# Attention's tensor part, its eviction and its use dealt out over successive steps, and left-over block products spread over three phases

## Chip, core and metric

One core of one Trainium2 chip. The metric is device time in microseconds (us) of one execution. The profiled span is some 2 us below the device time. An eviction is a read of matmul results out of PSUM, the memory that matmuls write to, by ACT or DVE; idle time before an instruction is shown in square brackets, with what ended it. Engines: PE (TensorE matmul), PEld (its weight loads), DVE (VectorE), ACT (ScalarE), SP (issues DMAs).

## The reference, cut to what matters

```python
# B=8 batches, H=8 heads, S=512 tokens, 32 states, D=64
scores  = scale * x @ state.T;  a  = softmax(scores);  xread = a @ state
scores2 = scale * state @ x.T;  a2 = softmax(scores2); sread = a2 @ x
x = concat([xread, sread], axis=2), laid out as (8 * 544, 512)
h = x @ w_in            # w_in 512 x 2048, 64-bit
g = h * cos(h)
return g @ w_out        # w_out 2048 x 512, 64-bit
```

## The kernel before

Instructions keep the order in which the program gives them, engine by engine; waits between engines are set from the tiles that instructions read and write. The main loop has 128 token steps (16 tiles of 128 hidden columns for each batch) and 16 steps for the states of all batches. In a step, `hidden` is two matmul calls into a PSUM buffer `h`, of which there are two. The gate follows: ACT (copy that adds a large constant, to round), DVE (`gate2`), ACT (Abs, sine; `gate3`), DVE (product, `gate4`).

The output product of two batches is done as seven block products in place of eight, in four phases of eight steps. One product per step goes into the MAIN half of an accumulator, in the fourth phase a fifth one into the SIDE half as well; the last two, `p7` and `p4`, are left over and go into the SIDE half during the next pair. Each tile's product follows its hidden matmul by three steps (`LAG`).

```python
at  = aps.tile([P, 2, S], F32, name="at")       # PSUM, attention
acc = ops.tile([P, 2, 2, S], F32, name="o")     # PSUM: MAIN, SIDE x 2 banks each

def tokens(self, k):                  # tensor part and eviction together
    for c in range(NC):
        self.turn_x(k, c, at[:, k % 2])
    nc.scalar.copy(self.xT[:, k], at[:, k % 2])
...
def output(t):
    if t.phase == 0:
        if product(MAIN, a11, t, i): keep_product(pr.u, MAIN)   # ACT reads MAIN
        if pr.before: p7(pr.before, i)                          # SIDE
    if t.phase == 1:
        last = product(MAIN, a12, t, i)
        if pr.before: p4(pr.before, i)                          # SIDE
        for ch in range(2 if last else 0):
            plus(pr.o, MAIN, ch, pr.u)                          # DVE reads MAIN
            ...
    # phase 2: MAIN alone.  phase 3: MAIN and SIDE, then the evictions
...
for step, t in enumerate(tiles()):    # conversions of weights cut
    hidden(t); gate(t); gate2(t); gate3(t)
    go(2 * s)                         # an attention part, whatever its engine
    if len(line) >= LAG: output(line.pop(0))
    gate4(t); sums(t)
    go(2 * s + 1)                     # the next attention part
    sums2(t)
```

The weights come as 64-bit numbers. Each of 20 blocks is turned into 32 bits by two ACT and four DVE instructions; 14 of them fall into steps 0 to 17.

## Time and profile before

| | before |
|---|---|
| device time, median of 3 runs | 955.45 us (951.56 to 956.37) |
| span profiled | 952.9 us |
| PE, DVE, ACT busy | 84%, 51%, 43% |
| mean granted PE clock | 0.951 |

PE is the fullest engine, but a share of busy time is an average. The prediction below shows the lines: the busy time of each stretch, the waits, and one wait as the timeline has it. The stretches are cut at the first hidden matmul of steps 0, 18, 32, 64, 96 and 128; steps 0 to 31 are pair 0, and so on by 32.

### The profile page before, as it was taken

Reading aid. Unit: us, or ns where it says so; the run is one execution under the profiler, and the core shown is the slowest. Engines: PE = TensorE matmul, PEld = TensorE weight load, DVE = VectorE, ACT = ScalarE, POOL = GpSimd, SP = SyncE. Lnnn points to the kernel's source line nnn. Section 1 sums busy time; section 2 is a strip of 40 time slices with the busy share of each in tenths; the row PEclk is TensorE's granted clock in tenths of the full one; section 3 lists DMA queues with packets and bytes.
Section 4 is the critical chain, followed back from the end, with each engine's and each line's share of the span. In section 5 each row is a group of like instructions: output and inputs, shape, how many; then the busy total and the mean of one; then the engine's idle time right before and its main releaser. Section 6 shows DMA issues by size and latency. Waiting matters only on the chain.

```text
span 952.9 us, 7331 instructions
## 1 busy us (share of the span) xinstructions
PE 797.4 (84%) x2720; PEld 350.9 (37%) x2720; DVE 482.4 (51%) x725; ACT 410.4 (43%) x634; POOL 3.1 (0%) x10
## 2 busy tenths in 40 slices
PE   3367667857998989689999899589989899899997
PEld 1133223323443434233433344234434343354454
DVE  2865866866644243756463326566442436643521
ACT  1555575554345424444444344543454335422312
POOL 1000000000000000000000000000000000000000
PEclk9879979989998999889999999799999999999999
DMA  5463223102000210202010301120000105001101
GB/s 132 150 182 133 90 87 88 22 1 45 0 14 10 41 26 1 44 1 45 0 23 0 67 1 22 23 44 1 11 11 1 22 1 133 1 0 23 22 10 35
DMA packets 110499, 37.17 MB, mean 39 GB/s; under 512 B 102464, under 2 KB 102464, under 8 KB 110464
## 3 DMA queue, kind: packets, MB, share of 16 engines
q1 hardware_dynamic: 109248, 36.19, 16.3%
q10 hardware_dynamic: 1088, 0.26, 0.2%
q8 instruction: 21, 0.34, 0.2%
q0 software_dynamic: 128, 0.26, 0.1%
q14 instruction: 14, 0.11, 0.0%
HBM read 27.79 MB, written 8.91 MB: 39 GB/s over the span
## 4 chain that ended last, share of the span: by engine, by line
PE 65%; DVE 19%; ACT 12%; issue 1%; DMA 1%; SPq 0%; DVEq 0%; ACTq 0%
PE o L464 33%; PE h L417 22%; PE at L274 4%; PE o L572 3%; DVE q L426 3%; ACT q L432 3%; DVE held L470 2%; ACT q L431 2%; DVE g_all L441 2%; DVE g_all L438 2%; PE at L354 1%; ACT q L423 1%; ACT xT L315 1%; DVE xT L293 1%; ACT L310 1%
## 5 line engine op out<-in xcount | busy, mean ns | idle before, releaser
L417 PE MATMUL h<-aT,sw 128*128 128x512 f32 x512 | 261.3, 635 | 9.6 <-ACT sw L386 7.9
L464 PE MATMUL o<-g_all,w_out 128*128 128x512 f32 x512 | 237.8, 604 | 6.1 <-ACT held L476 3.5
L426 DVE SCALAR_TENSOR_TENSOR q<-q,h 128x512 f32<-128x512 f32 (+1 forms) x144 | 93.9, 652 | 253.3 <-ACT q L423 253.0
L423 ACT ACTIVATE q<-h 128x512 f32<-128x512 f32 (+1 forms) x144 | 82.4, 572 | 274.6 <-PE h L417 274.6
L464 PE MATMUL o<-g_all,s 128*128 128x512 f32 x384 | 176.9, 596 | 3.5 <-ACT held L476 2.7
L431 ACT ACTIVATE q<-q 128x512 f32<-128x512 f32 (+1 forms) x144 | 87.3, 606 | 179.2 <-DVE q L426 179.2
L438 DVE TENSOR_TENSOR g_all<-h,q 128x512 f32<-128x512 f32 (+1 forms) x144 | 94.8, 658 | 132.0 <-ACT q L432 131.9
L417 PEld LDWEIGHTS h<-aT,sw 128*128 128x128 f32 x512 | 98.6, 202 | 136.5 <-issue 111.4
L464 PEld LDWEIGHTS o<-g_all,w_out 128*128 128x128 f32 x512 | 97.0, 195 | 130.3 <-issue 117.3
L464 PEld LDWEIGHTS o<-g_all,s 128*128 128x128 f32 x384 | 71.3, 191 | 92.8 <-issue 85.0
L432 ACT ACTIVATE q<-q,halfpi 128x512 f32<-128x512 f32 (+1 forms) x144 | 100.5, 698 | 4.5
L274 PE MATMUL at<-w_in,stT 64*32 64x512 f32 (+1 forms) x512 | 42.3, 705 | 54.1 <-ACT xT L315 41.7
L441 DVE TENSOR_TENSOR g_all<-g_all 128x512 f32<-128x512 f32 x128 | 83.2, 688 | 3.2
L470 DVE SCALAR_TENSOR_TENSOR held<-o,held 128x512 f32<-128x512 f32 x40 | 25.9, 687 | 41.8 <-PE o L464 41.5
L386 ACT COPY sw<-at 128x1024 f32<-128x1024 f32 (+1 forms) x32 | 31.6, 987 | 24.9 <-PE at L274 24.9
L572 PE MATMUL o<-w_out,g_all 128*128 128x512 f32 x64 | 31.3, 621 | 6.4 <-DVE w_out L221 4.1
L274 PEld LDWEIGHTS at<-w_in,stT 64*32 64x32 f32 x512 | 6.4, 112 | 80.1 <-ACT xT L315 47.5
L417 PE MATMUL h<-sT,w_in 128*128 128x256 f32 x128 | 30.2, 379 | 0.0
L417 PEld LDWEIGHTS h<-sT,w_in 128*128 128x128 f32 x128 | 24.3, 190 | 10.1 <-issue 6.7
L249 PE MATMUL at<-ident,x_b 128*128 128x128 f32 x112 | 17.6, 281 | 10.5 <-ACT xT L256 6.3
L249 PEld LDWEIGHTS at<-ident,x_b 128*128 128x128 f32 x112 | 13.9, 144 | 27.7 <-ACT xT L256 12.1
L488 DVE STREAM_TRANSPOSE ot<-held 128x512 f32<-128x512 f32 x32 | 22.3, 696 | 1.3 <-DMA out_dram<-ot 1.2
(72 smaller groups left out, 397.5 us busy)
## 6 DMA issues: line engine op xcount, KB each, us to landing
out_dram<-ot SPq DMA_DIRECT2D x136, 64.0 KB, 2.0
x_b<-in_x_dram SPq DMA_DIRECT2D x32, 256.0 KB, 4.4
g_all<-in_moe_w_out_dram SPq DMA_DIRECT2D x8, 1024.0 KB, 4.9
g_all<-in_moe_w_in_dram SPq DMA_DIRECT2D x6, 1024.0 KB, 5.1
g_all<-in_moe_w_in_dram SPq DMA_DIRECT2D x4, 512.0 KB, 7.3
x_b<-in_moe_w_out_dram SPq DMA_DIRECT2D x1, 1024.0 KB, 5.8
xT<-in_moe_w_out_dram SPq DMA_DIRECT2D x1, 1024.0 KB, 7.9
s<-in_state_dram ACTq DMA_DIRECT2D x4, 64.0 KB, 5.2
```

The costliest lines, as they stand in the source:

```text
L274: nc.tensor.matmul(out=(to[j] if to else at[:, j])[Ns * k:Ns * k + Ns, 0:n], lhsT=w[D * j:D * j + D, self.b, Ns * k:Ns * k + Ns], rhs=r(sl ...
L386: nc.scalar.copy(sw_of[self.b, nt][:, :, c0:c1], at[:, :, 0:c1 - c0])
L417: nc.tensor.matmul(out=t.hp, lhsT=t.lhs(i), rhs=t.rhs(i), start=(i == 0), stop=(i == t.kn - 1))
L423: nc.scalar.activation(t.q, t.hp, func=ACTF.Copy, bias=MAGIC)
L426: nc.vector.scalar_tensor_tensor(out=t.q, in0=t.q, scalar=MAGIC, in1=t.hp, op0=ALU.subtract, op1=ALU.subtract)
L431: nc.scalar.activation(t.q, t.q, func=ACTF.Abs)
L432: nc.scalar.activation(t.q, t.q, func=ACTF.Sin, bias=halfpi, scale=-TWO_PI)
L438: nc.vector.tensor_tensor(t.g, t.hp, t.q, op=ALU.mult)
L441: nc.vector.tensor_tensor(out, a, b, op=ALU.subtract)
L464: nc.tensor.matmul(out=acc[:, bank, ch], lhsT=w[:, i, P * ch:P * ch + P], rhs=g.g, start=(i == 0), stop=(i == NH - 1))
L470: nc.vector.scalar_tensor_tensor(out=out[:, ch], in0=acc[:, bank, ch], scalar=TWO_PI, in1=b[:, ch], op0=ALU.mult, op1=ALU.add)
L572: nc.tensor.matmul(out=acc[:, MAIN, i], lhsT=t.g[:, P * i:P * i + P], rhs=w_out[:, :, t.f, :], start=(n == 0), stop=(n == NF - 1))
```

## The change

Its intent: attention's matmuls, the evictions of their results and their use go into different lists, so that each stands at a fitting place of a step (matmuls ahead of `hidden`, an eviction behind the first gate instruction, vector work in the hole while ACT computes) and the use comes a step or more later. The left-over products are popped from a list in two of three steps of phases 0 to 2, in place of every step of phases 0 and 1. Cut to its core:

```diff
         def tokens(self, k):
             for c in range(NC):
                 self.turn_x(k, c, at[:, k % 2])
+
+        def tokens_kept(self, k):
             nc.scalar.copy(self.xT[:, k], at[:, k % 2])
...                                    # turn, keep3 and products alike
+        def products(self, nt, bank=None, c0=0, c1=WC):
+            to = at if bank is None else acc[:, bank]     # pair 0: SIDE is idle
...
         if t.phase == 0:
             if product(MAIN, a11, t, i):
+                pr.u = Held()
                 keep_product(pr.u, MAIN)
-            if pr.before:
-                p7(pr.before, i)
         if t.phase == 1:
-            last = product(MAIN, a12, t, i)
-            if pr.before:
-                p4(pr.before, i)
-            for ch in range(2 if last else 0):
-                plus(pr.o, MAIN, ch, pr.u)
-                store(2 * pr.n, 0, ch, pr.o)
+            if product(MAIN, a12, t, i):
+                o = Held()
+                for ch in range(2):
+                    plus(o, MAIN, ch, pr.u)
+                store(2 * pr.n, 0, o)
...
         if t.phase == 3:
-            last = product(MAIN, s2, pr.b[0, i], i)
+            if product(MAIN, s2, pr.b[0, i], i):
+                for ch in range(2):
+                    plus(pr.u, MAIN, ch, pr.u)
             free(pr.b[0, i])
-            product(SIDE, s4, t, i)
+            if product(SIDE, s4, t, i):
+                ...                                       # plus SIDE, total, store
             free(t)
+        elif pr.before and (t.phase * NH + i) % 3 < 2:
+            pr.before.more(1)                             # SIDE
...
+        go(0)                          # attention on PE
         hidden(t)
         gate(t)
         gate2(t)
+        go(1)                          # evictions on ACT, early
+        go(3)                          # attention on DVE, in the gate's hole
         gate3(t)
-        go(2 * (step % NF))
-        if len(line) >= LAG:
-            output(line.pop(0))
         gate4(t)
         sums(t)
-        go(2 * (step % NF) + 1)
+        go(2)                          # evictions and exponentials on ACT, late
+        go(4)                          # attention on DVE, late
         sums2(t)
+        if len(line) >= LAG:
+            output(line.pop(0))
```

More of the change, by code (lines that the diff above doesn't have):

```diff
@@ L83 @@
     x_b = consts.tile([P, NC, H, D], F32)
-    held = consts.tile([P, 3, 2, S], F32)
+    NHELD = 3
+    held = consts.tile([P, NHELD, 2, S], F32)
+    held_free = list(range(NHELD))
     st = s1.rearrange("p f d -> p (f d)")[:, 0:B * 2 * D]
@@ L119, with states, states_kept @@
     at = aps.tile([P, 2, S], F32, name="at")
-    def states(half):
+    def states(half, to):
         for i in range(4):
-            nc.tensor.transpose(out=at[:, half, P * i:P * i + P],
+            nc.tensor.transpose(out=to[:, P * i:P * i + P],
                                 in_=st[:, 4 * half + i, :], identity=ident)
+    def states_kept(half, to):
         dst = slice(4 * half, 4 * half + 4)
-        src = at[:, half].rearrange("p (b m) -> p b m", b=4)
+        src = to.rearrange("p (b m) -> p b m", b=4)
         nc.vector.tensor_scalar(stT[:, dst], src, 1.0 / TWO_PI, None,
@@ L341, in turn, with turn_kept @@
                                     identity=ident)
+        def turn_kept(self, j):
             nc.scalar.copy(self.a2T[:, j].rearrange("p c m -> p (c m)"),
@@ L373, in keep2, with keep3 @@
                                 identity=ident)
+        def keep3(self):
             nc.scalar.activation(
@@ L377, in keep2, with products_kept @@
                 func=ACTF.Copy, scale=1.0 / TWO_PI)
-        def products(self, nt, c0=0, c1=WC):
+        def products(self, nt, bank=None, c0=0, c1=WC):
+            to = at if bank is None else acc[:, bank]
+            cols = slice(WC * nt + c0, WC * nt + c1)
+            self.per_head(stT, lambda rows, k: w_in[rows, k, cols], c1 - c0,
+                          [to[:, j] for j in range(2)])
+        def products_kept(self, nt, bank=None, c0=0, c1=WC):
+            to = at if bank is None else acc[:, bank]
             if c0 == 0:
                 sw_of[self.b, nt] = swp.tile([P, 2, WC], F32, name="sw")
-            cols = slice(WC * nt + c0, WC * nt + c1)
-            self.per_head(stT, lambda rows, k: w_in[rows, k, cols],
-                          n=c1 - c0)
-            nc.scalar.copy(sw_of[self.b, nt][:, :, c0:c1], at[:, :, 0:c1 - c0])
-        def first_products(self, n):
-            to = [acc[:, 0, j] for j in range(2)]
-            self.per_head(stT, lambda rows, k: w_in[rows, k, 0:n], n, to)
-            sw_of[self.b, 0] = swp.tile([P, 2, WC], F32, name="sw")
-            for j in range(2):
-                nc.scalar.copy(sw_of[self.b, 0][:, j, 0:n], to[j][:, 0:n])
-        def scores1(self):
-            self.scores()
-            self.max1()
+            nc.scalar.copy(sw_of[self.b, nt][:, :, c0:c1], to[:, :, 0:c1 - c0])
     attn = {}
@@ L441, in minus, with more, __init__, done @@
         nc.vector.tensor_tensor(out, a, b, op=ALU.subtract)
+    MAIN, SIDE = 0, 1
     class Pair:
         def __init__(self, n, before):
-            self.n, self.before = n, before
-            self.b = {}
-            x, y, z = before.at_ if before else (1, 2, 0)
-            self.at_ = z, x, y
-            self.u = held[:, z]
-            self.p5, self.o = held[:, x], held[:, y]
+            self.n, self.before, self.b = n, before, {}
+            self.left = [(p7, i) for i in range(NH)] + [
+                (p4, i) for i in range(NH)]
+        def more(self, n):
+            for _ in range(n):
+                if self.left:
+                    p, i = self.left.pop(0)
+                    p(self, i)
+    class Held:
+        def __init__(self):
+            self.n, self.uses = held_free.pop(0), 2
+            self.t = held[:, self.n]
+        def done(self):
+            self.uses -= 1
+            if self.uses == 0:
+                held_free.append(self.n)
     def product(bank, w, g, i):
@@ L469, in plus @@
     def plus(out, bank, ch, b):
-        nc.vector.scalar_tensor_tensor(out=out[:, ch], in0=acc[:, bank, ch],
-                                       scalar=TWO_PI, in1=b[:, ch],
+        nc.vector.scalar_tensor_tensor(out=out.t[:, ch], in0=acc[:, bank, ch],
+                                       scalar=TWO_PI, in1=b.t[:, ch],
                                        op0=ALU.mult, op1=ALU.add)
@@ L475, in keep_product, with total, store, go @@
         for ch in range(2):
-            nc.scalar.activation(out[:, ch], acc[:, bank, ch], func=ACTF.Copy,
+            nc.scalar.activation(out.t[:, ch], acc[:, bank, ch], func=ACTF.Copy,
                                  scale=TWO_PI)
-    def total(out, a, b, ch):
-        nc.vector.tensor_tensor(out[:, ch], a[:, ch], b[:, ch], op=ALU.add)
     later = []
-    def store(b, half, ch, src):
-        def go():
+    def total(out, a, b):
+        for ch in range(2):
+            later.append(lambda ch=ch: nc.vector.tensor_tensor(
+                out.t[:, ch], a.t[:, ch], b.t[:, ch], op=ALU.add))
+    def store(b, half, src):
+        def go(ch):
             ot = osb.tile([P, S], F32, name="ot")
             nc.vector.transpose(out=ot.rearrange("p (j i) -> p j i", i=32),
-                                in_=src[:, ch].rearrange("p (j i) -> p j i",
-                                                         i=32))
+                                in_=src.t[:, ch].rearrange(
+                                    "p (j i) -> p j i", i=32))
             rows = out[b * T:b * T + S, :].rearrange("(j t) d -> t j d", t=32)
@@ L497, in go @@
                         "p (j i) -> p j i", i=32))
-        later.append(go)
+            src.done()
+        later.extend([lambda: go(0), lambda: go(1)])
     def sums(t):
@@ L516, in free @@
         g_free.append(t.slot)
-    MAIN, SIDE = 0, 1
     def p7(pr, i):
@@ L522, in p7 @@
         free(pr.b[2, i])
-        for ch in range(2 if last else 0):
-            plus(pr.u, SIDE, ch, pr.u)
-        for ch in range(2 if last else 0):
-            total(pr.p5, pr.u, pr.p5, ch)
-            store(2 * pr.n + 1, 1, ch, pr.p5)
+        if last:
+            for ch in range(2):
+                plus(pr.u, SIDE, ch, pr.u)
+            total(pr.p5, pr.u, pr.p5)
+            store(2 * pr.n + 1, 1, pr.p5)
     def p4(pr, i):
@@ L531, in p4 @@
         free(pr.b[1, i])
-        for ch in range(2 if last else 0):
-            plus(pr.u, SIDE, ch, pr.u)
-            store(2 * pr.n, 1, ch, pr.u)
+        if last:
+            for ch in range(2):
+                plus(pr.u, SIDE, ch, pr.u)
+            store(2 * pr.n, 1, pr.u)
     def output(t):
@@ L542, in output @@
             if product(MAIN, a11, t, i):
+                pr.u = Held()
                 keep_product(pr.u, MAIN)
-            if pr.before:
-                p7(pr.before, i)
         if t.phase == 1:
-            last = product(MAIN, a12, t, i)
-            if pr.before:
-                p4(pr.before, i)
-            for ch in range(2 if last else 0):
-                plus(pr.o, MAIN, ch, pr.u)
-                store(2 * pr.n, 0, ch, pr.o)
+            if product(MAIN, a12, t, i):
+                o = Held()
+                for ch in range(2):
+                    plus(o, MAIN, ch, pr.u)
+                store(2 * pr.n, 0, o)
         if t.phase == 2:
             if product(MAIN, s1, pr.b[0, i], i):
+                pr.p5 = Held()
                 keep_product(pr.p5, MAIN)
         if t.phase == 3:
-            last = product(MAIN, s2, pr.b[0, i], i)
+            if product(MAIN, s2, pr.b[0, i], i):
+                for ch in range(2):
+                    plus(pr.u, MAIN, ch, pr.u)
             free(pr.b[0, i])
-            product(SIDE, s4, t, i)
-            free(t)
-            for ch in range(2 if last else 0):
-                plus(pr.u, MAIN, ch, pr.u)
-            for ch in range(2 if last else 0):
-                total(pr.o, pr.u, pr.p5, ch)
-                plus(pr.o, SIDE, ch, pr.o)
-                store(2 * pr.n + 1, 0, ch, pr.o)
+            if product(SIDE, s4, t, i):
+                o = Held()
+                for ch in range(2):
+                    plus(o, SIDE, ch, pr.p5)
+                total(o, o, pr.u)
+                store(2 * pr.n + 1, 0, o)
+            free(t)
+        elif pr.before and (t.phase * NH + i) % 3 < 2:
+            pr.before.more(1)
     def state_output(t):
@@ L576, in state_output @@
         free(t)
-        for i in (2 * n, 2 * n + 1):
-            if i < NH:
-                p7(pr, i)
-            elif i < NF:
-                p4(pr, i - NH)
+        pr.more(2)
         if n == NF - 1:
@@ L621 @@
     a0.all_tokens()
-    states(0)
+    states(0, at[:, 0])
+    states_kept(0, at[:, 0])
     a0.scores()
@@ L638 @@
     a0.norm1()
-    a0.first_products(HC)
+    a0.products(0, MAIN, 0, HC)
+    a0.products_kept(0, MAIN, 0, HC)
     a0.max2()
+    convert0(2)
     a0.exp2()
-    convert0(2)
     convert1(2)
-    states(1)
     convert0(3)
-    convert1(3)
-    def slots_of(b):
-        E = [(b + 1, "tokens", k) for k in range(NK)] + [
-            (b + 1, n) for n in ("scores1", "max2", "spread1", "shift",
-                                 "exps", "sums", "spread1", "norm1")]
-        L = [(b + 1, n, j) for n in ("turn", "reads") for j in range(2)] + [
-            (b + 1, "keep"), (b + 1, "keep2")]
-        if b == 0:
-            L0 = [(0,) + p[1:] for p in L]
-            at_ = {1: (0, "products", 0, HC, WC), 7: (0, "products", 1),
-                   14: (0, "products", 2), 22: (0, "products", 3),
-                   27: (1, "products", 0)}
-            at_.update(zip((2, 3, 4, 5, 6, 8), L0))
-            at_.update(zip((10, 11, 12, 13, 16, 17, 18, 19, 20, 21, 23, 24), E))
-            at_.update(zip((25, 26, 28, 29, 30, 31), L))
-            return at_
-        at_ = {1: (b, "products", 1), 11: (b, "products", 2),
-               18: (b, "products", 3), 26: (b + 1, "products", 0)}
-        at_.update(zip((2, 3, 4, 5, 6, 7, 8, 9, 10, 12, 13, 14), E))
-        at_.update(zip((15, 16, 19, 20, 21, 22), L))
-        return {k: p for k, p in at_.items() if p[0] < B}
@@ new lines, with plan, prod, pairs @@
+    convert2(2)
+    convert3(2)
+    def plan(b):
+        pe, x_act, y_act, x_dve, y_dve = [
+            {s: [] for s in range(NF)} for _ in range(5)]
+        def prod(s, b, nt, *bank):
+            pe[s].append((b, "products", nt) + bank)
+            x_act[s].append((b, "products_kept", nt) + bank)
+        def pairs(s, b, name, kept, i):
+            pe[s] += [(b, name, i), (b, name, i + 1)]
+            x_act[s].append((b, kept, i))
+            y_act[s].append((b, kept, i + 1))
+        def early(b, s):
+            pairs(s[0], b, "tokens", "tokens_kept", 0)
+            pairs(s[1], b, "tokens", "tokens_kept", 2)
+            pe[s[2]].append((b, "scores"))
+            x_dve[s[2]].append((b, "max1"))
+            y_dve[s[2]].append((b, "max2"))
+            x_dve[s[3]].append((b, "spread1"))
+            y_dve[s[3]].append((b, "shift"))
+            y_act[s[4]].append((b, "exps"))
+            x_dve[s[5]].append((b, "sums"))
+            y_dve[s[5]].append((b, "spread1"))
+            x_dve[s[6]].append((b, "norm1"))
+        def late(b, s):
+            pairs(s[0], b, "turn", "turn_kept", 0)
+            pe[s[1]].append((b, "reads", 0))
+            pe[s[2]].append((b, "reads", 1))
+            x_dve[s[2]].append((b, "keep"))
+            pe[s[3]].append((b, "keep2"))
+            x_act[s[3]].append((b, "keep3"))
+        if b == 0:
+            prod(1, 0, 0, SIDE, HC, WC)
+            prod(3, 0, 1, SIDE)
+            prod(7, 0, 2, SIDE)
+            prod(11, 0, 3, SIDE)
+            prod(13, 1, 0, SIDE)
+            late(0, (1, 2, 3, 4))
+            early(1, (5, 6, 7, 8, 9, 10, 11))
+            late(1, (12, 13, 14, 15))
+        else:
+            prod(0, b, 1)
+            prod(7, b, 2)
+            prod(11, b, 3)
+            if b + 1 < B:
+                prod(13, b + 1, 0)
+                early(b + 1, (1, 2, 3, 4, 5, 6, 7))
+                late(b + 1, (8, 9, 10, 12))
+        return pe, x_act, y_act, x_dve, y_dve
@@ L687 @@
     LAG = 3
-    line, slots = [], {}
+    line = []
     for step, t in enumerate(tiles()):
-        if step % NF == 0:
-            slots = slots_of(t.b) if t.b < B else {}
+        s = step % NF
+        if s == 0 and t.b < B:
+            steps = plan(t.b)
+        todo = [p[s] if t.b < B else [] for p in steps]
         def go(n):
-            if n in slots:
-                part(*slots[n])
-            if later:
-                later.pop(0)()
+            for p in todo[n]:
+                part(*p)
         conv = conv_at.get(step)
@@ L702 @@
             fetch(N_LOADS + 2)
+        if step != 1:
+            go(0)
+        if step == 4:
+            states(1, acc[:, SIDE, 1])
         hidden(t)
+        if step == 0:
+            convert1(3)
+            convert2(3)
+            convert3(3)
+            convert0(conv)
+        if step == 1:
+            go(0)
         if conv is not None:
-            if step:
-                convert1(conv)
-                convert2(conv)
+            convert1(conv)
+            convert2(conv)
         gate(t)
         gate2(t)
+        go(1)
         if conv is not None:
-            if step == 0:
-                convert2(3 - 1)
-                convert3(3 - 1)
-                convert0(conv)
-                convert2(3)
-                convert3(3)
-                convert1(conv)
-                convert2(conv)
             convert3(conv)
+        go(3)
         gate3(t)
+        if later:
+            later.pop(0)()
+        gate4(t)
+        if t.pair is not None:
+            sums(t)
+        if step == 4:
+            states_kept(1, acc[:, SIDE, 1])
+        go(2)
         nxt = conv_at.get(step + 1)
@@ L723 @@
             convert0(nxt)
-        go(2 * (step % NF))
+        go(4)
+        if step in block_at:
+            blocks(*block_at[step])
+        if t.pair is not None:
+            sums2(t)
         if len(line) >= LAG:
             output(line.pop(0))
-        gate4(t)
-        if t.pair is not None:
-            sums(t)
-        if step in block_at:
-            blocks(*block_at[step])
-        go(2 * (step % NF) + 1)
-        if t.pair is not None:
-            sums2(t)
         line.append(t)
```

## The prediction

> **What bounds the kernel now.** I read the views in this order: busy times, waits, busy time by stretch, then the timeline where a wait is longest. The first line of the page says that TensorE (PE) is the engine to look at, and that it is not full.
>
> ```profile
> PE 797.4 (84%) x2720; PEld 350.9 (37%) x2720; DVE 482.4 (51%) x725; ACT 410.4 (43%) x634; POOL 3.1 (0%) x10
> ```
>
> PE lacks 155 us of the 952.9 us span, and some of its busy time is spent at a reduced clock. To place this, I cut the span at the first hidden matmul (L417) of every second batch; a pair of batches is one round of the seven block products. The rows are: lead-in, pairs 0 to 3, and the tail with the state tiles.
>
> ```profile
> 0.00:35.41 35.41, 11.10 (x57) 5.26 (x57) 15.53 (x23) 8.81 (x16) 3.14 (x10) 1.00 0.52 133
> 35.41:258.90 223.49, 161.33 (x597) 66.61 (x596) 150.51 (x208) 120.40 (x172) 0.00 (x0) 0.89 0.27 78
> 258.90:462.68 203.78, 181.57 (x627) 77.49 (x626) 97.69 (x151) 88.31 (x136) 0.00 (x0) 0.95 0.12 21
> 462.68:663.97 201.29, 179.10 (x627) 76.58 (x626) 97.57 (x151) 88.31 (x136) 0.00 (x0) 0.97 0.12 21
> 663.97:844.47 180.50, 168.79 (x538) 71.67 (x537) 87.39 (x135) 78.45 (x121) 0.00 (x0) 0.99 0.11 24
> 844.47:952.90 108.43, 95.52 (x281) 53.34 (x279) 33.73 (x62) 26.15 (x54) 0.00 (x0) 0.97 0.11 20
> ```
>
> After the length come the busy times of PE, weight loads, DVE, ACT and POOL, then PE's granted clock. In pairs 1 to 3 DVE and ACT are busy less than half of the time, so waiting, not their throughput, keeps PE idle. In pair 0 the weight conversions bring DVE to 150 of 223 us and the clock to 0.89. The list of waits (total, count, longest) names what PE waits for:
>
> ```profile
> PE at L274 <- ACT xT L315: 41.7, 7, 8.7
> PE at L371 <- DVE sr L365: 17.1, 7, 3.0
> PE at L339 <- ACT xT L342: 12.0, 5, 4.8
> ```
>
> All three are attention's. Its tensor instruction stands in the same step as, or half a step behind, the eviction or the vector work that it needs, in the one buffer `at`, and what follows on PE waits too. The costliest case, in pair 2:
>
> ```profile
> 594.96 1.88 PE L464 MATMUL o<-g_all,s 128*128 128x512 f32 x4
> ...
> 601.82 1.28 ACT L310 ACT_TABLE_LOAD   x1
> ...
> 603.11 1.06 ACT L310 ACTIVATE aT<-aT 128x1024 f32<-128x1024 f32 x1
> ...
> 605.56 1.96 PE L274 MATMUL at<-w_in,stT 64*32 64x512 f32 x16 [8.72 <-ACT xT L315]
> ```
>
> The product of w_in (L274) comes straight behind the exponentials, which queue on ACT behind the gate and a table load: 8.72 us idle, after which L274 itself takes 1.96 us in place of 1.09. Finally, the four phases of pair 2, eight tiles each:
>
> ```profile
> 462.68:515.41 52.73, 48.78 (x166) 20.88 (x164) 26.52 (x38) 24.69 (x37) 0.00 (x0) 0.97 0.06 10
> 515.41:566.74 51.33, 47.12 (x168) 20.27 (x167) 15.93 (x28) 19.69 (x31) 0.00 (x0) 1.00 0.18 31
> 566.74:616.67 49.93, 41.21 (x145) 17.42 (x144) 25.45 (x39) 23.10 (x35) 0.00 (x0) 0.90 0.14 22
> 616.67:663.97 47.30, 41.99 (x155) 18.00 (x154) 29.67 (x49) 20.83 (x33) 0.00 (x0) 1.00 0.12 23
> ```
>
> The third has the least PE work (one product per tile, not two), yet takes as long: it is set by attention's chain through DVE and ACT.
>
> **What the Trainium skill says.** "TensorE: Matmul & The Clock Gate", Part 1 (The HAM clock gate): after an idle window of about 3.4 us the array falls to half clock. The trace agrees: behind the 8.72 us gap L274 is 1.8 times as long. Its Part 2 (Step-by-step) says that only weight loads are pulled ahead while matmuls stay in program order, and "Architectural detail" that ACT and DVE are strict FIFO; hence one waiting matmul stops PE, and moving instructions is the cure. It agrees with the gap above, where ready hidden matmuls stood behind L274. "Perfetto Trace Analysis", Optimization Strategy, advises interleaving regimes that have different limits; spreading the left-over products is that. "ScalarE: Activation LUTs", What ACT_TABLE_LOAD costs, gives 1283 ns plus about 1380 ns of drain. The load is 1283 ns here too, but the exponential starts at 603.11, 0.01 us behind its end, and the load starts within 0.02 us of the sine before it, so no drain is added.
>
> **The change, part by part.** The order of instructions shows the same work: 1464 matmul calls, the same vector instructions, 16 table loads on both sides, one ACT copy fewer. So the sum is over waits alone.
>
> *PE's floor.* With nothing in the way a matmul instruction of 512 columns takes 0.43 us: in the timeline a step of 12 of them repeats every 5.15 us (488.40 to 493.55). A steady pair has 32 tiles x 4 hidden = 128 and 7 products x 8 tiles x 4 = 224 such instructions: 352 x 0.429 = 151 us. Attention of two batches adds about 21.7: products and scores 10 x 1.15 (clean steps with one take 6.26 to 6.37 in place of 5.15), token transposes 8 x 0.49, reads 4 x 1.05, turns 4 x 0.47, and 0.3. Floor: **172.7 us**.
>
> *Pair 2*, 201.3 now: 28.6 over the floor. Part one removes the waits by construction: tensor part ahead of the hidden matmuls, first copy between the gate's first and third ACT instructions, vector work in the hole that DVE has while ACT runs Abs and sine (0.63 + 0.72 = 1.35 us), use a step later. The exponentials now sit at step 5 and the next product in `at` at step 7, a whole step later. Part two makes the first three phases even: from steps of 3.43 and 5.15 us to 1.72 + 1.72 + 2/3 x 1.72 = 4.58, while DVE there needs about 2.06 (gate and difference) plus up to 2.6 to 3.0 of attention. That nearly balances, with one tile of slack. I leave 2 us per batch for the exponentials and for sw copies used one step later: 172.7 + 4.6 = 177.3, so **24 saved**. *Pair 1*: 203.8 to 178, **26 saved**.
>
> *Pair 3* has one batch of attention and three products: 151 + 10.9 + 3.5 = 165.4, plus 3 = 168.5 in place of 180.5: **12 saved**.
>
> *Pair 0* has no left-over products, so part two gives nothing. In a step with a conversion I expect a cycle that ACT and DVE share: two ACT conversions 2.25, the rest of the three DVE conversions that began in the second of them (2.6 - 1.1 = 1.5), gate 0.7, Abs and sine 1.5: 6.0 us. Fourteen such, four others at 4.6, exponentials and copies 8: 110. Steps 0 to 17 take 137.8 now. Walking the new order step by step with the measured durations put the end of tile 17 only 26 us earlier, as the first steps stay slow; I take 26. In steps 18 to 31, 86 us now, DVE sets about 34 (six steps at 5.1 with block differences and attention, and 3 for the exponentials) and PE 47: 81, **5** more. Pair 0: **31 saved**.
>
> *Tail*: the final additions of phase 3 now follow the gate, and the first SIDE sum no longer stands ahead of the MAIN ones; of the 2.3 us stall at the ninth-batch start I count **3 saved** with its clock. Lead-in: its order changes, but its gain is in pair 0's walk: 0. Sum 31 + 26 + 24 + 12 + 3 = 96; 952.9 - 96 = 857. Measured times lie 2.5 us above the span (955.45 against 952.9): **859 us**.
>
> **Rivals.** (1) The wait moves. Two products per batch (steps 7 and 11) are copied to sw in the step just before their use, and each copy lengthens ACT's chain by 1.0 us; if PE waits 1 us at each, or `at` is still held by the exponentials at step 7, pairs 1 to 3 give back 15 to 20: about 877. For it: two hidden buffers allow only one tile of slack. Against: a tile's gate needs 3.5 us from its last hidden matmul, while PE has 5.15 us of other work before it needs the buffer. (2) DVE and ACT bound pair 0, so its conversions eat all of the gain: about 885 to 890. For it: 150 us of DVE in this pair, and no SIDE products to move. Against: both engines still idle a third of it, and in the longest steps (17.2 and 13.0 us) PE waits for exponentials, not for conversions. (3) The balance matters more than the waits: PE stays warm everywhere and comes within 1 us per batch of its floor, with pair 0 near 180: about 842. (4) Nothing moves, as a transfer was the limit: DMA engines are busy 12% in pairs 1 to 3, so I give it almost nothing.
>
> **Range and chances.** Pairs 1 to 3 could give 45 to 72, pair 0 between 15 and 45, the tail 0 to 5. Not all go one way: low 838, high 882. Even rival 2 is 7% faster; slower by 2% would need a new stall longer than all those removed. Faster 0.97, same 0.02, slower 0.01.
>
> **What would show it.** The row of pair 2 should be 175 to 181 us long with PE's clock above 0.98; phases 1 and 2 shorter by about 1.72 us per tile moved, the third not longer than now. The waits of L274, L371 and L339 should fall below 10 us together in pairs 1 to 3. Pair 0 should be near 192 us, with DVE over 75% busy. I am wrong on part one if PE's idle time in pair 2 stays above 10 us under other names (sw copies, the hidden buffer), on part two if the third phase is still limited by DVE, and on pair 0 if it stays above 210 or falls under 180.

## The result, and the profile after

929.35 us (928.72 to 929.63, 4 runs) against 954.36: ratio 0.9739, 95% interval 0.9711 to 0.9767. A ratio is the mean time of one kernel's runs over the mean of the other's of the same rounds, so not quite the ratio of the medians quoted. The gain is 25 us where 96 were predicted. The predicted range, 838 to 882, does not hold it.

The same stretches in the changed kernel, pairs 0 to 3 and the tail (columns as in the prediction: length, busy PE, PEld, DVE, ACT, POOL, PE's clock, DMA):

```profile
32.45:253.43 220.98, 163.88 (x615) 69.72 (x615) 152.49 (x212) 121.51 (x177) 0.00 (x0) 0.89 0.27 82
253.43:445.58 192.15, 178.23 (x634) 76.04 (x626) 97.66 (x151) 86.32 (x136) 0.00 (x0) 0.98 0.13 22
445.58:638.17 192.59, 178.66 (x634) 76.06 (x627) 97.66 (x151) 86.31 (x136) 0.00 (x0) 0.98 0.13 22
638.17:820.66 182.49, 170.48 (x529) 72.75 (x522) 86.66 (x133) 77.89 (x121) 0.00 (x0) 0.97 0.11 23
820.66:926.94 106.28, 93.83 (x281) 52.75 (x279) 34.16 (x62) 26.21 (x54) 0.00 (x0) 0.98 0.11 20
```

Pairs 1 and 2 became about 12 and 9 us shorter, pair 3 even 2 us longer, and pair 0 stayed nearly where it was. In pair 2 PE is still idle for 13.9 us (192.6 - 178.7). The list of waits after (total, count, longest) says for what:

```profile
PE o L481 <- DVE held L487: 24.7, 11, 3.8
...
PE at L362 <- ACT xT L350: 16.1, 8, 4.8
...
PE o L280 <- ACT held L493: 13.7, 1, 13.7
...
PE o L481 <- ACT sw L400: 6.4, 4, 1.6
...
PE o L481 <- ACT held L493: 6.2, 3, 2.1
...
PE at L280 <- ACT xT L321: 4.8, 1, 4.8
```

The exponentials' wait of before, 41.7 us, is down to 4.8 (the last line). In its place stand waits of the accumulator `o`: for `held` (L487 and L493, the evictions of a finished product) and for `sw` (L400, the copy of attention's product of w_in). With one more of 4.1 us for `stT` (the transposed states) they make 55 us. Where the largest group comes from, the timeline shows in the row of pair 2, where the products of pair 1's last phase end, three steps behind their tiles (step 66; start, duration, engine, line, operation; PE's two products are MAIN and SIDE of the same step):

```profile
459.54 1.88 PE L481 MATMUL o<-g_all,s 128*128 128x512 f32 x4
...
463.11 1.28 DVE L487 SCALAR_TENSOR_TENSOR held<-o,held 128x512 f32<-128x512 f32 x2
...
464.45 2.92 PE L481 MATMUL o<-g_all,s 128*128 128x512 f32 x4 [3.03 <-DVE held L487]
...
467.30 1.78 PE L280 MATMUL at<-xT,stT 64*32 64x512 f32 x16
```

MAIN ends at 461.4. The SIDE product does not start behind it, but waits until DVE has read MAIN, and DVE gets to this only behind the gate of the running step. The gap also costs clock: the same four matmuls take 2.92 us in place of 1.88, and L280 1.78 in place of 1.09 (e1 below). The step takes 11.2 us, where the same step without this wait takes 6.3 in e1.

The longest single wait stands in pair 0 (step 10):

```profile
115.81 1.22 DVE L225 CUSTOM_DVE_ANT_0 w_in<-w_in,s 128x2048 uint16<-128x2048 uint16 x1
...
118.50 1.06 ACT L493 ACTIVATE held<-o 128x512 f32<-128x512 f32 x2
...
119.62 1.96 PE L280 MATMUL o<-w_in,stT 64*32 64x512 f32 x16 [13.72 <-ACT held L493]
```

Attention's product of w_in goes into the idle SIDE half, but waits for ACT's reading of MAIN, which stands in ACT's queue behind the exponentials and a conversion. Not all of the 13.7 us is due to that: the product also needs its block of w_in, whose conversion (L225) ends at 117.03, only 2.6 us before the product starts.

Nothing in the arithmetic asks for a wait on the other half: SIDE and MAIN are different banks, with different users. So the theory, **T**: the program's waits treat the accumulator tile as one, so that a matmul into either half waits for whatever reads of the other half the program gives before it. The change then added waits, since it moved such reads ahead of SIDE products. The rival, **R**: the waits are real needs of the products, of the block tiles or of the accumulators, and would come back under other names.

### The profile page after: what moved, and what is told of

Read it like the earlier page. It is cut to its first block, busy times and chain, and to the rows that moved or that the text cites. A ratio compares the mean times of both kernels' runs of the same rounds, so it can differ in the third digit from the quotient of the medians.

```text
span 926.9 us, 7339 instructions
## 1 busy us (share of the span) xinstructions
PE 795.3 (86%) x2720; PEld 351.7 (38%) x2720; DVE 483.2 (52%) x725; ACT 404.6 (44%) x633; POOL 3.1 (0%) x10
## 4 chain that ended last, share of the span: by engine, by line
PE 68%; DVE 15%; ACT 13%; issue 1%; DMA 1%; SPq 0%; ACTq 0%; DVEq 0%
PE o L481 32%; PE h L419 24%; PE at L280 4%; DVE q L428 3%; ACT q L434 3%; PE o L593 3%; ACT q L433 3%; ACT q L425 2%; PE at L362 2%; DVE g_all L440 2%; PE at L253 1%; DVE g_all L443 1%; DMA x_b<-in_x_dram 1%; DVE xT L299 1%; DVE held L487 1%
## 5 line engine op out<-in xcount | busy, mean ns | idle before, releaser
L481 PE MATMUL o<-g_all,w_out 128*128 128x512 f32 x512 | 242.6, 608 | 28.1 <-DVE held L487 11.3
L419 PE MATMUL h<-aT,sw 128*128 128x512 f32 x512 | 256.9, 626 | 1.2 <-ACT sw L400 0.7
L481 PE MATMUL o<-g_all,s 128*128 128x512 f32 x384 | 179.1, 601 | 13.4 <-DVE held L487 13.4
L419 PEld LDWEIGHTS h<-aT,sw 128*128 128x128 f32 x512 | 94.8, 199 | 127.8 <-issue 103.5
L280 PE MATMUL at<-w_in,stT 64*32 64x512 f32 x432 | 30.3, 618 | 7.6 <-ACT xT L321 4.8
L280 PE MATMUL o<-w_in,stT 64*32 64x512 f32 (+1 forms) x96 | 11.2, 677 | 28.8 <-DVE w_in L225 15.1
L487 DVE SCALAR_TENSOR_TENSOR held<-o,held 128x512 f32<-128x512 f32 x40 | 25.7, 684 | 16.4 <-PE o L481 16.4
L362 PE MATMUL at<-x_b,xT 128*64 128x128 f32 x256 | 19.3, 297 | 16.1 <-ACT xT L350 16.1
L400 ACT COPY sw<-at 128x1024 f32<-128x1024 f32 x27 | 27.2, 1006 | 0.0
L362 PEld LDWEIGHTS at<-x_b,xT 128*64 128x64 f32 x256 | 15.1, 147 | 28.5 <-ACT xT L350 22.4
```

Source lines behind the costliest of these rows:

```text
L280: nc.tensor.matmul(out=(to[j] if to else at[:, j])[Ns * k:Ns * k + Ns, 0:n], lhsT=w[D * j:D * j + D, self.b, Ns * k:Ns * k + Ns], rhs=r(sl ...
L362: nc.tensor.matmul(out=at[rows, 0, cols], lhsT=self.a2T[:, j, c, rows], rhs=x_c[:, j, k:k + 2], start=(c == 0), stop=(c == NC - 1), tile_p ...
L419: nc.tensor.matmul(out=t.hp, lhsT=t.lhs(i), rhs=t.rhs(i), start=(i == 0), stop=(i == t.kn - 1))
L481: nc.tensor.matmul(out=acc[:, bank, ch], lhsT=w[:, i, P * ch:P * ch + P], rhs=g.g, start=(i == 0), stop=(i == NH - 1))
L487: nc.vector.scalar_tensor_tensor(out=out.t[:, ch], in0=acc[:, bank, ch], scalar=TWO_PI, in1=b.t[:, ch], op0=ALU.mult, op1=ALU.add)
```

## Experiments

The kernels of one call ran on the same chip; there were three calls on three chips (e1 to e4; e5 to e8; e9 to e11), in which before took 954.4, 954.5 and 952.8 us, so rows of different calls compare to about 0.2%; the change itself was measured in an earlier one. All gave the right result except e7, which is wrong on purpose. The time is the median; the lengths of the stretches, in us, are those of the one profiled execution, from the first hidden matmuls in its timeline (pair 0 in two parts):

| kernel | time | ratio to before | lead-in | steps 0-17 | steps 18-31 | pair 1 | pair 2 | pair 3 | tail |
|---|---|---|---|---|---|---|---|---|---|
| before | 954.4 | 1 | 35.4 | 137.8 | 85.7 | 203.8 | 201.3 | 180.5 | 108.4 |
| the change | 929.4 | 0.974 | 32.4 | 136.7 | 84.3 | 192.1 | 192.6 | 182.5 | 106.3 |
| e1 change, accumulator split | 882.2 | 0.922 | 31.5 | 130.9 | 84.6 | 179.7 | 179.7 | 167.6 | 105.8 |
| e2 before, accumulator split | 946.5 | 0.991 | 34.3 | 135.7 | 88.4 | 200.9 | 200.3 | 181.3 | 104.2 |
| e3 change, SIDE product first | 890.7 | 0.933 | 32.4 | 136.8 | 84.3 | 179.7 | 179.7 | 169.3 | 107.0 |
| e4 spread alone | 947.1 | 0.991 | 35.5 | 139.0 | 85.8 | 197.9 | 198.0 | 182.4 | 105.8 |
| e5 separation alone, split | 887.7 | 0.930 | 31.4 | 130.2 | 83.5 | 183.7 | 183.9 | 167.7 | 105.8 |
| e6 spread alone, split | 929.5 | 0.974 | 34.5 | 137.2 | 88.8 | 192.5 | 193.7 | 176.8 | 105.9 |
| e7 light conversion (wrong result) | 851.3 | 0.892 | 29.6 | 111.9 | 82.0 | 179.7 | 179.7 | 167.6 | 99.5 |
| e8 e1, copies early | 856.7 | 0.897 | 31.1 | 120.1 | 78.6 | 175.3 | 175.3 | 165.9 | 105.9 |
| e9 change, copies early | 907.8 | 0.952 | 32.2 | 129.1 | 80.2 | 188.5 | 190.1 | 181.2 | 106.3 |
| e10 e8, products behind `hidden` | 843.5 | 0.885 | 31.3 | 114.4 | 75.8 | 173.9 | 173.9 | 166.7 | 105.8 |
| e11 e10, conversions moved | 837.3 | 0.878 | 31.1 | 114.8 | 76.7 | 173.9 | 173.9 | 166.7 | 99.5 |

### e1: the accumulator as two tiles

```diff
-    acc = ops.tile([P, 2, 2, S], F32, name="o")
+    acc_main = ops.tile([P, 2, S], F32, name="om")
+    acc_side = ops.tile([P, 2, S], F32, name="os")
+    # acc[:, bank, ...] picks the tile; nothing else changes
```

> Edit: the accumulator of the changed kernel, one tile with a MAIN and a SIDE half, becomes two tiles; nothing else. Theory T (halves of one PSUM tile are tied by the waits of the program: a matmul into SIDE waits for the vector or scalar reads of MAIN that stand ahead of it, and the other way round): the waits 'PE o <- DVE held' at the phase ends (3.0 to 3.8 us each), 'PE o <- ACT held' 13.7 us in pair 0, 'PE o <- DVE stT' 4.15 us and 'PE o <- ACT sw' 1.6 us vanish; pairs 1 to 3 about 180, 180 and 167 us long (192.2, 192.6, 182.5 now), pair 0 about 200 (221 now), time about 865. Rival R (the waits are real needs, of the accumulators or of the block tiles): the same waits stay under other names and the time is within 1% of 929.

882.21 us (874.88 to 883.16). T holds for pairs 1 to 3 to within a microsecond: 179.7, 179.7 and 167.6 against the expected 180, 180 and 167. Pair 0 lost only 5.5 us in place of 21, and so the time is 882 and not 865. The long wait of step 10 shows why. Its share for the conversion stays, under its own name, as R would have it (from e1's list of waits; the longest, 8.4 us, is step 10's):

```profile
PE os L288 <- DVE w_in L233: 13.4, 3, 8.4
```

The program itself shows what the split does. PE's order at step 34, the end of phase 3 of pair 0, with the engine for which each matmul waits; first the change, then e1:

```
L481 Matmult o<-g_all,s_94 128x512 x2            (MAIN)
L481 Matmult o<-g_all,s_95 128x512 [waits DVE]   (SIDE)

L489 Matmult om<-g_all,s_94 128x512 x2           (MAIN)
L489 Matmult os<-g_all,s_95 128x512 x2           (SIDE, no wait)
```

And the timeline of e1 at step 66, to be held against the one above:

```profile
440.64 1.88 PE L489 MATMUL om<-g_all,s 128*128 128x512 f32 x4
...
442.35 1.88 PE L489 MATMUL os<-g_all,s 128*128 128x512 f32 x4
...
444.21 1.28 DVE L495 SCALAR_TENSOR_TENSOR held<-om,held 128x512 f32<-128x512 f32 x2
```

SIDE follows MAIN 1.71 us later, at full speed, and DVE reads MAIN at leisure. In pair 2 PE is now busy 174.4 of 179.7 us, with the clock at its full rate (the stretches of pairs 1 and 2 in e1):

```profile
247.01:426.68 179.67, 174.35 (x634) 75.71 (x626) 97.50 (x151) 86.31 (x136) 0.00 (x0) 1.00 0.14 24
426.68:606.36 179.68, 174.36 (x635) 75.72 (x627) 97.52 (x151) 86.31 (x136) 0.00 (x0) 1.00 0.14 24
```

### e2: the same split in the kernel before

> Edit: the same split of the accumulator in the kernel before. Theory T: before had only a few such waits (ACT held 1.2 us three times and 2.7, DVE held 0.9 four times and 2.3, and clock lost behind them), so 10 to 20 us gained, about 940: the tie costs the changed order far more than the old one. Rival (the split is simply worth some 60 us to any order): about 890. Rival R: 954, no change.

946.49 us: 8 us gained, a little under the 10 to 20 of T and far from the other two. The old order had the tie too, but few reads of MAIN stood ahead of SIDE products. It cost the new order 47.

### e3: one tile, but the SIDE product ahead of the evictions

```diff
-            if product(MAIN, a12, t, i):
-                ...plus(o, MAIN, ...)
-        elif pr.before and (t.phase * NH + i) % 3 < 2:
-            pr.before.more(1)
+        last = product(MAIN, w, g, i)
+        if pr.before and (t.phase * NH + i) % 3 < 2:
+            pr.before.more(1)
+        if last and t.phase == 1:
+            ...plus(o, MAIN, ...)          # phases 0, 2 and 3 likewise
```

> Edit: the changed kernel with its one accumulator tile, but at a phase end the SIDE product is put ahead of the evictions of MAIN (as the kernel before had it); what reads MAIN is unchanged. Theory T: the phase-end waits in pairs 1 to 3 vanish by order alone, these pairs as in e1 (180, 180, 167), pair 0 as it is now (about 220), time about 888. Rival R: a real need of the SIDE product is not met by order: time within 1% of 929.

890.72 us, expected 888. Order alone does it: pairs 1 and 2 are 179.7 us, as with two tiles (pair 3 169.3, against 167.6), and pair 0 is untouched, where the tie comes from attention's products. At step 66 MAIN and SIDE now run in one piece, in one tile:

```profile
447.17 3.60 PE L481 MATMUL o<-g_all,s 128*128 128x512 f32 x8
...
450.81 1.29 DVE L487 SCALAR_TENSOR_TENSOR held<-o,held 128x512 f32<-128x512 f32 x2
```

So the SIDE product needs nothing from those evictions, and for pairs 1 to 3 R falls: two different edits, one leaving the waits' rules and one leaving the order, remove the same time. In pair 0 R was right in part, as step 10 shows.

### e4, e5, e6: each part of the change alone

e4 has the change's block products with the old attention and step order, on the one tile. e5 and e6 have one part each on two tiles. e5 differs from e1 by one condition; e6 is e4 with the split of e1:

```diff
-        elif pr.before and (t.phase * NH + i) % 3 < 2:
+        elif pr.before and t.phase < 2:           # e5: left-overs as before
             pr.before.more(1)
```

> Edit: the changed kernel's block products (left-over ones spread over three phases, free list of held tiles), with the attention and the step order of the kernel before. If the spread by itself is the gain: below 940. Theory T: attention's waits stay and the phase-end waits come in, so about 945 to 960, no clear gain.

> Edit: accumulators as two tiles (as in e1), attention separated and dealt out as in the change, but the left-over products back in phases 0 and 1 alone. With e1 (882) and e2 (946) this gives the worth of each part without the tie. Expected: the separation is the larger part; the third phase loses the spread, pairs 1 to 3 about 6 to 8 us longer than e1 each, time about 902. If the spread is what counts: above 925.

> Edit: accumulators as two tiles, left-over products spread over three phases, attention and step order as before the change. Expected: the exponentials' wait of 4 to 5 us with the cold stretch behind it stays once per batch, pairs about 192, time about 930. If attention's separation adds little on top of the spread: below 900.

On two tiles, from 946.5: the spread alone gives 17 us, the separation alone 59, both 64. The spread adds 5.5 us to the separation, 4 us in each of pairs 1 and 2 and nothing in pair 3: less than the 20 that the text for e5 gave it. In pair 2, from e5 to e1, the first two phases became 5.1 us shorter together and the third 1.8, but the fourth 2.7 longer; why it is not more, no run shows. The times of e4 and e6 came out as expected. They differ by the tile alone: the tie costs the spread on its own 17.6 us (947.1 against 929.5), against 8 in the kernel before, so the rewritten block products raise it. How the separation takes it to 47, no run splits up.

### e7: is pair 0 set by the conversions?

```diff
     def convert1(i):
+        return                       # two of four vector instructions out
     def convert2(i):
+        return                       # the third out
...
-        nc.vector.tensor_tensor(dst, dst, e.bitcast(I32), op=ALU.add)
+        nc.vector.tensor_tensor(dst, dst, e, op=ALU.subtract)
```

> Wrong result on purpose. Edit on e1: of the four vector instructions that turn a 64-bit weight block into 32 bits, the first three (2.6 us per block) are left out, the fourth becomes a subtraction of the same size, so that only finite values arise. Question: why pair 0 did not shorten. If the conversions set the pace there (the prediction's cycle of 6.0 us, of which 1.5 us would go 14 times): steps 0 to 17 fall from 131 us to 112 or less. If instead PE's attention at half clock, waiting for copies queued behind the gate and the exponentials, sets it: steps 0 to 17 stay at 122 or more. Steps 18 to 31 (84.6) and pairs 1 to 3 (179.7, 179.7, 167.6) unchanged either way.

Steps 0 to 17 fell from 130.9 to 111.9 us (e1, then e7):

```profile
31.50:162.44 130.94, 94.27 (x362) 40.81 (x363) 95.08 (x128) 83.55 (x118) 0.00 (x0) 0.86 0.42 126
29.56:141.48 111.92, 87.30 (x362) 37.85 (x363) 57.05 (x80) 82.96 (x118) 0.00 (x0) 0.91 0.46 141
```

So the conversions do stand in the path, by 19 of the 21 us that the cycle of the prediction gives them (14 x 1.5). Steps 18 to 31, expected unchanged, fell by 2.6 us too, and the tail, which has two conversions, by 6.3. But 111.9 us without them is still far from the 89 that this cycle leaves (110 - 21). The two alternatives of the text were not exclusive; the next runs show the second.

### e8 and e9: the second copy early

```diff
             x_act[s].append((b, kept, i))
-            y_act[s].append((b, kept, i + 1))     # behind the sine
+            x_act[s].append((b, kept, i + 1))     # behind the gate's first copy
```

> Edit on e1: the second of each pair of copies out of the attention buffer (tokens, turned weights) also goes early on ACT, behind the gate's first instruction, in place of behind the sine. Theory: the reads and the next tokens wait for that copy (18.4 and 11.6 us idle in e1, and clock lost behind it), so 10 to 25 us gained, most of it in pair 0: 858 to 872. Rival: 0.57 us more in the gate's chain of eight steps per pair eats it, and pair 0 waits for ACT and DVE anyway: within 5 us of 882.

> Edit: the changed kernel with its one accumulator tile, only the second copy of each pair early (as in e8). If the copies and the tie are separate losses, this takes about the same 25 us as on the split accumulators: about 904. If the tie hides the copies' waits, under 10 us: above 919.

e8 took 856.7 us: 25 us below e1, just past the good end of the range. The waits that it was aimed at, in e1 and then in e8:

```profile
PE at L370 <- ACT xT L358: 18.4, 8, 5.8
...
PE at L261 <- ACT xT L270: 11.6, 4, 4.9
```

```profile
PE at L370 <- ACT xT L358: 3.8, 1, 3.8
PE at L261 <- ACT xT L270: 2.3, 2, 1.6
```

24 us of these waits are gone; 10.8 us of the gain lie in steps 0 to 17, 6 in steps 18 to 31, 4.4 in each of pairs 1 and 2. On the one tile e9 took 907.77 us, 22 us less than the change (expected about 25), so it is a separate loss from the accumulator's tie. The change had put these copies behind the sine, the gate's last ACT instruction, so PE's next use of the buffer waited for the step's whole gate.

### e10 and e11: two more moves

```diff
-        go(0)                        # e10: attention's products ...
         hidden(t)
+        ...products                  # ... behind the hidden matmuls
...
-        go(2)                        # e11: exponentials
         convert0(nxt)                #      conversion first
+        go(2)
```

In e11 the two tail steps with a conversion also give the state product ahead of it.

> Edit on e8 (857): the products of w_in stand behind the hidden matmuls of their step instead of ahead of them, so that PE has these to do while the exponentials or a conversion are awaited. In pair 0 the waits of 8.4 us (step 10, a conversion) and 4.3 us (step 22, the exponentials) should fall by a hidden matmul's 1.7 to 3.4 us each: 849 to 855. Rival: the sw copy then comes later and the next hidden matmuls wait for it: 857 to 865.

> Edit on e10: the next conversion's ACT part also goes ahead of the exponentials, and in the two tail steps with a conversion the state product goes ahead of it (2.06 us wait twice, and a cold stretch). Expected: 3 us in pair 0 and 5 us in the tail less than e10, so about 845. Rival: ACT merely changes which of its users waits: as e10.

e10: 843.54, better than expected; 5.7 us in steps 0 to 17 and 2.8 in steps 18 to 31, 1.4 in each of pairs 1 and 2. e11: 837.31. Its tail gave 6.3 us, as expected (5). Its other move gave nothing: steps 0 to 17 took 114.8 against 114.4, and steps 18 to 31 76.7 against 75.8, so there its rival was right. At a ratio of 0.878 this is the fastest version, 12% below before and 10% below the change as it was.

## Why the prediction was wrong

**Pairs 1 to 3: the floor was right, the wait in the new order was missed.** The text said that part one "removes the waits by construction", and left 2 us per batch for the exponentials and sw copies (it then added 4.6 for two batches, not 4). Predicted were 178, 177 and 168.5; measured 192.1, 192.6 and 182.5; with the tie cut (e1) 179.7, 179.7 and 167.6, and in e10 173.9 for pairs 1 and 2, where the floor was put at 172.7. The missing term is the wait of a SIDE product for the eviction of MAIN that now stands ahead of it: 12.4 + 12.9 + 14.9 = 40 us. In pair 2 some 9 us of it is idle time (3.0 + 3.8 + 2.1) and the rest, 4 us, the clock: PE is busy 178.7 us for the work that takes 174.4 in e1. Rival 1, that the wait moves, was right in kind, but named the wrong ones (sw copies, `at`) and half the size. The diff showed the swap of eviction and product; the prediction has no word on it, nor on the program's waits. The kernel before already had the sign: in its list of waits `PE o L464 <- ACT held L476`, four waits of a block product behind evictions, 6.2 us together. Three of them, 1.2 us each, go with the split (e2); the fourth, 2.7 us, stays and is no sign of the tie.

**Pair 0: the cycle was too short.** 192 us were predicted, 221 measured, 215.5 without the tie. The failed step is "a cycle that ACT and DVE share": it puts 110 us on steps 0 to 17, where PE is taken as always in time. The runs take 136.7 us there, of which 5.8 go with the tie (e1), 10.8 with the copies early (e8), and 5.7 with the products behind the hidden matmuls (e10): down to 114.4, near the 112 that the prediction came to (137.8 - 26). So the conversions' part on DVE was sized about right (19 of 21 us, e7), and PE's waits in series with it, at a mean clock of 0.87, were left out. Rival 2 had the right result for pair 0, but for a reason that e7 and e8 share out between conversions and copies. What the text held against it, that the longest steps wait for exponentials and not for conversions, does not hold in e1: 8.4 us at step 10 are for a conversion, which itself stood behind the exponentials on ACT.

**Tail and lead-in.** 3 us predicted for the tail, 2.1 came; 0 for the lead-in, 3.0 came. The 2.5 us between span and time are a median less the span of another run; the run profiled took 954.7 us, 1.8 above its span.

**The signs named beforehand.** Waits of L274, L371 and L339 (now L280, L379, L345) did fall below 10 us in pairs 1 to 3, to 1.4, and in pair 2 the third phase did not get longer (48.8 us, 49.9 before). The row of pair 2 missed its 175 to 181 us, and DVE in pair 0 was busy 69%, not over 75%. Pair 0 above 210 us said that the cycle was wrong, as it was. PE's idle time in pair 2 of 13.9 us (limit 10) was to speak against part one; but part one gives 59 us once the tie is cut (e5), and it was the order of evictions in the rewritten block products that the sum had missed. The two corrections, 40 us in pairs 1 to 3 and 29 in pair 0, make about the difference between 859 and 929.

## What to carry to other kernels

Before a reordering is judged, list for each matmul what the built program makes it wait for: two halves of one PSUM tile may be tied though their banks differ, and then an eviction that moves ahead of a product into the other half can become a stall. Give accumulators with different users separate tiles; here one declaration was worth 47 us. When a cycle is estimated, put the engine that is not the bound into it as well: a copy late in one engine's queue is late by all that stands before it.

## What stays open

The runs show that the waits follow the declaration of the tile, not by which rule they are set. The attention buffer `at` has two halves as well. It is tied likewise: in the program built from the changed kernel, the token transposes of step 34 into its first half wait for ACT's copy out of the second. e8 puts these second copies early; how much of its 25 us is the tie and how much a real need, no run separates. What still holds steps 0 to 17 at 114 us, beyond the conversions, was not measured.

## What the Trainium skill lacked or had wrong

- "TensorE: Matmul & The Clock Gate", Part 1: it gives an idle window of about 3.4 us before the clock falls. The page's table "Why this matters for your kernels" has about 3 us as the limit for gaps. Neither tells what a gap near it costs: here one of 3.03 us between matmuls (3.86 between weight loads) was enough at step 66, where the four matmuls behind it took 2.92 us in place of 1.88; behind an equal gap at step 34 they took 1.98. A gap of 2.08 us (step 74) cost that step 2.3 us in all, so hardly any clock.
- "ScalarE: Activation LUTs", What ACT_TABLE_LOAD costs: the load of 1283 ns is confirmed; the drain of about 1380 ns is not, as the exponential starts 0.01 us behind the load's end (601.82 + 1.28, then 603.11, in the kernel before).
- None of the pages says that waits can be coarser than a bank. Here a matmul into one half of a four-bank PSUM tile waited for reads of the other half, at step 66 for 3.03 us; with two tiles in its place the kernel was 47 us faster (e1).
